# Output products of a gated layer: one issue list with fixed offsets, VectorE sums and some plain products

## The chip, the cores and the metric

One core of a Trainium2 chip runs the whole program. The metric is the device time of one execution in microseconds (us); less is better. Matrix products run on TensorE (PE, with its weight loads as PEld), elementwise work on VectorE (DVE), ScalarE (ACT) and GpSimd (POOL); SyncE (SP) issues nearly all DMAs, in program order.

## The reference

```python
x = attention with k and v averaged over blocks of 8          # 2304 tokens x 512
x = sum over e of p[:, e] * (relu(x @ w1[e]) @ w2[e])         # 4 experts, 512 -> 1024 -> 512
xn = x / sqrt(mean(x * x) + 1e-6) * rms_g
g = xn @ w_gate; val = xn @ w_val                             # 512 -> 1536
out = ((g * sigmoid(g)) * val) @ w_out                        # 1536 -> 512
```

All in float32. `w_gate`, `w_val` and `w_out` come as 64-bit words, which the kernel turns into float32 first.

## The kernel before

The 2304 tokens are three passes of 768. First come three expert stages (one for each pass, 8 quads each), then three gated stages (12 quads each: g and v for each of six rows of 256 hidden units). A quad (`quad`, L432) is a product of 2x2 blocks in Winograd's form of Strassen's scheme, with seven products instead of eight. Each float32 operand is split into a high and a low part, and a product is three matmuls (high by high, high by low, low by high), so a quad is seven steps of six 384-column matmuls. After each step the quad calls `hook`, which issues a share of everything else: gates, preparation of the next quad's weights, norms, conversions and DMAs. So the order on every in-order engine is written out by hand, a step at a time.

The PSUM tile qX is written at steps 0, 2, 4 and 6. Between them ACT copies it (L458, L461) and DVE adds it into `u` (L465). `gate_after` and `val_after` (L500, L521) leave four 384-column blocks of the gated value for each row in a tile `qq`.

The output product takes two rows at a time, also in Winograd's form: `products` (L548) forms the operands and `second_g` (L618) issues 14 units of six matmuls (M1, M2, M6, M7, M5, M4, M3, two halves each), 84 matmuls in all. M1, M2 and M3 use blocks of `qq` as they are (`rows`, L559). M6, M7, M5 and M4 need sums t1 and t2 (L580, L588, L591), which run on POOL. For the last pair they run on DVE and M3 is moved forward. Each operand is rounded to its high part on ACT (L562, L568), and DVE subtracts that to give the low part (L564, L569). M1's operand is formed at the end of the pair's second v quad, and the units follow evenly over the next 28 steps; those of the very last pair come after the last quad. Results are added into SBUF (`put_x` L636 and `put_y` L643 on DVE; on ACT, L634 and L641, for a pass's first pair), and L629 stores them.

The last expert product of the third pass (72 matmuls of 512 columns, `second`, L705, with sums at L727) is spread over the first four gated quads. `norm` (L749) then reads the sums back from DRAM (L765), scales them (L772), turns them on PE (L782) and stores them for the gated stages.

In pass 0 `prep_w` (L253) makes each gated quad's weights on POOL, ACT and DVE from a block loaded one quad ahead (L250) and stores them; later passes load them (L264, L265).

The conversion of the 64-bit weights (`convert_all`, L321) runs in the background of the expert stages. Each block is loaded to a tile `cr` (L336), with tag `rw` or `kr` by turns. For each of the six rows of `w_out`, `combine` (L382) makes seven weight blocks in high and low parts: sums on POOL (L387 to L390), high parts on ACT (L396), low parts on DVE (L399). `put` queues the store to `ws_d`, which SP issues two steps later (L241). The first four blocks lie in tiles of tags `aT` and `kr`, one buffer each, so the next load into `kr` waits until those stores have landed. `load_gw` (L537) reads `ws_d` back, into four buffers `w2` (L542).

Of the kernel before, what the change touches and what calls it, by code (L numbers as in the profile page):

```python
# [54 lines left out]
def tile_kernel(ctx: ExitStack, tc, qp, kp, vp, dp, w1r, w2r, w64, rg, out):  # L55
# [265 lines left out]
    def convert_all():  # L321
# [4 lines left out]
        halves = {}  # L326
# [15 lines left out]
        for n, (k, r_, c) in enumerate(keys):  # L342
# [39 lines left out]
    def combine(r, halves):  # L382
# [42 lines left out]

# [119 lines left out]

    M1, M2, M6, M7, M5, M4, M3 = range(7)

    def products(p, g, tail):  # L548

        qs = [gate_t.pop((p, 0, g * G + j)) for j in range(G)]  # L550
        eng = nc.vector if tail else nc.gpsimd
        ops = {}
        late_t = {}

        def new_op(n, tag, bufs):
            ops[n] = late["sb"].tile([P, 2, G, N], F32R, name="ho", tag=tag, bufs=bufs)
            return ops[n]

        def rows(n, k, tag="hA", bufs=4):  # L559
            o = new_op(n, tag, bufs)  # L560
            for j in range(G):
                nc.scalar.activation(o[:, 0, j], qs[j][:, k], AF.Copy)  # L562
            for j in range(G):
                nc.vector.tensor_tensor(o[:, 1, j], qs[j][:, k], f32(o[:, 0, j]), op=ALU.subtract)  # L564

        def sums(n, src):
            o = new_op(n, "hA", 4)
            nc.scalar.activation(o[:, 0], src, AF.Copy)  # L568
            nc.vector.tensor_tensor(o[:, 1], src, f32(o[:, 0]), op=ALU.subtract)  # L569

        def new_t():
            return late["sb"].tile([P, 2, G, N], F32, name="ht", tag="hB", bufs=3)

        def steps():
            rows(M1, 1)
            yield
            rows(M2, 3)
            t1 = new_t()
            for j in range(G):
                eng.tensor_tensor(  # L580
                    t1[:, :, j], qs[j][:, 0:1].to_broadcast([P, 2, N]), qs[j][:, 1:3], op=ALU.subtract
                )
            yield
            rows(M3, 2, "hB", 3)
            yield
            t2 = new_t()
            for j in range(G):
                eng.tensor_tensor(t2[:, 0, j], qs[j][:, 2], t1[:, 0, j], op=ALU.subtract)  # L588
            yield
            for j in range(G):  # L590
                eng.tensor_tensor(t2[:, 1, j], qs[j][:, 3], t2[:, 0, j], op=ALU.subtract)  # L591
            yield
            yield
            sums(M6, t2[:, 0])
            for _ in range(4):
                yield
            sums(M7, t1[:, 1])
            for _ in range(4):
                yield
            sums(M5, t1[:, 0])  # L600
            for _ in range(4):
                yield
            sums(M4, t2[:, 1])
            yield

        it = steps()
        next(it)

        def need(n):
            while n not in ops:  # L610
                next(it)
            return ops[n]

        return it, need

    ct = {}

    def second_g(p, g, need, tail):  # L618

        first, last = g == 0, g == R2 // G - 1  # L620
        x2 = late["pg"].tile([P, 2, 512], F32, name="gx", tag="gx")[:, :, :N]
        y2 = None
        if first:
            ct[0] = new_y(1).rearrange("p (j c n) -> p j c n", j=2, c=2)

        def out_of(i, j):
            if last:
                o = out[i * 256:(i + 1) * 256, p * TT * P + j * N:p * TT * P + (j + 1) * N]
                nc.sync.dma_start(o.rearrange("(c p) n -> p c n", c=2), ct[i][:, j])  # L629

        def put_x(i, j, fresh, z=None):
            d, z = ct[i][:, j], x2 if z is None else z
            if fresh and first:
                nc.scalar.activation(d, z, AF.Copy)  # L634
            else:
                nc.vector.tensor_tensor(d, z, d, op=ALU.add)  # L636

        def put_y(i, j, c, fresh, z):
            d = ct[i][:, j, c]
            if fresh and first:  # L640
                nc.scalar.activation(d, z, AF.Copy)  # L641
            else:
                nc.vector.tensor_tensor(d, z, d, op=ALU.add)  # L643

        order = (M1, M2, M3, M6, M7, M5, M4) if tail else (M1, M2, M6, M7, M5, M4, M3)
        for n in order:
            o = need(n)
            if n == M6 and first:
                ct[1] = new_y(0).rearrange("p (j c n) -> p j c n", j=2, c=2)
            if n in (M2, M7):  # L650
                y2 = [late["ps"].tile([P, 512], F32, name="gy", tag="py", bufs=2)[:, :N] for _ in range(2)]
            if n == M3 and tail:
                z2 = [late["ps"].tile([P, 512], F32, name="gz", tag="qX", bufs=2)[:, :N] for _ in range(2)]
            for c in range(2):
                w = gw[p, g, n // 2]
                z = y2[c] if n in (M2, M7, M4) else z2[c] if n == M3 and tail else x2[:, c]
                start = n in (M1, M2, M7) or n == M3 and tail
                for j in range(G):
                    wh, wl = (w[:, n % 2, j, i, c * P:(c + 1) * P] for i in range(2))
# [7 lines left out]
                elif n == M7:  # L667
                    put_y(1, 1, c, True, z)
                elif n == M4:
                    put_y(1, 0, c, False, z)  # L670
                elif n == M3 and tail:
                    put_y(0, 1, c, True, z)
                elif c:
# [606 lines left out]
```

## Time and profile before

| | |
|---|---|
| Median of 3 runs | 1314.22 us (1312.6 to 1317.47) |
| Profiled execution: time, span | 1311.7 us, 1309.9 us |
| PE, PEld busy | 1253.0 us (96%), 1152.8 us (88%) |
| DVE, ACT, POOL busy | 829.0 us (63%), 539.9 us (41%), 339.9 us (26%) |
| Mean granted TensorE clock | 0.987 of full speed |
| DMA | 342.27 MB, mean 261 GB/s |

The span runs from the first instruction to the last; the execution's own time has about 2 us around it. A matmul's duration is longer than the interval at which matmuls start, since they are pipelined, so that PE's busy time counts work that overlaps. Idle time of PE, and stretches at a lower clock, are what can be lost or won beside the number of matmuls.

### The profile page before, as it was taken

The page shows a single profiled execution, that of the slowest core. Times are in us where ns is not written, and L with a number is a line of the kernel's source. Part 1 is how long each engine was busy: PE and PEld are TensorE (multiplying, and loading weights), DVE is VectorE, ACT ScalarE, POOL GpSimd, SP SyncE. Part 2 cuts the span into 40 slices and gives each one's busy share as a digit, 9 for nine tenths or more (in the row PEclk, how much of TensorE's full clock was granted, in tenths as well). Part 3 has the DMA queues.
Part 4 walks back from the last instruction along what each step waited for, and adds up shares of the span by engine and source line. Part 5 has one row for each costly group of instructions (what it writes and reads, how often), then busy time and mean ns, then how long its engine had stood idle before and what let it go on. Part 6 is the DMA issues. An engine that isn't in the chain of part 4 may idle for free.

```text
span 1309.9 us, 18235 instructions
## 1 busy us (share of the span) xinstructions
PE 1253.0 (96%) x6836; PEld 1152.8 (88%) x6836; DVE 829.0 (63%) x1323; ACT 539.9 (41%) x1246; POOL 339.9 (26%) x301
## 2 busy tenths in 40 slices
PE   7899999999999999999998999999999999999995
PEld 6788898889888889889897888898988999999994
DVE  5864555557556665455766666567779556865655
ACT  5664444435443333233433332355454344433330
POOL 5234324310132222100332432134352022202200
PEclk8899999999999999999999999999999999999999
DMA  7296787768777776557979886667887776757651
GB/s 241 88 350 254 267 284 273 278 236 322 272 287 278 267 266 235 199 217 265 334 289 317 297 290 238 251 249 281 306 322 272 295 281 258 297 202 287 235 209 64
DMA packets 94135, 342.27 MB, mean 261 GB/s; under 512 B 9312, under 2 KB 32864, under 8 KB 73696
## 3 DMA queue, kind: packets, MB, share of 16 engines
q1 hardware_dynamic: 93712, 339.94, 71.3%
q10 hardware_dynamic: 336, 1.18, 0.3%
q8 instruction: 53, 0.87, 0.3%
q14 instruction: 34, 0.28, 0.1%
HBM read 238.33 MB, written 102.76 MB: 260 GB/s over the span
## 4 chain that ended last, share of the span: by engine, by line
PE 44%; DVE 8%; DMA 4%; issue 1%; ACT 1%; SPq 0%; POOL 0%; DVEq 0%; ACTq 0%; POOLq 0%
PE qX L453 5%; PE qX L455 5%; PE qX L454 5%; PE py L716 4%; PE py L717 4%; PE py L715 4%; PE qY L453 2%; PE qY L454 2%; PE qY L455 2%; DVE ho L564 2%; PE gx L663 2%; DMA ws_d<-oh 1%; DMA wt<-wt_d 1%; PE gx L664 1%; PE gx L662 1%; PE gy L663 1%
## 5 line engine op out<-in xcount | busy, mean ns | idle before, releaser
L727 DVE SCALAR_TENSOR_TENSOR y<-py,dps,y 128x512 f32<-128x512 f32 x126 | 94.5, 750 | 190.6 <-PE py L717 190.2
L371 POOL TENSOR_TENSOR cx<-cx,ca 128x512 f32<-128x512 f32 x36 | 49.2, 1367 | 394.8 <-DVE ca L369 166.5
L453 PE MATMUL qX<-xos,wt 128*128 128x384 f32 x336 | 116.3, 346 | 3.6 <-ACT qZ L458 2.6
L455 PE MATMUL qX<-xos,wt 128*128 128x384 f32 x336 | 114.3, 340 | 0.0
L717 PE MATMUL py<-w,hB 128*128 128x512 f32 x288 | 114.0, 396 | 0.0
L716 PE MATMUL py<-w,hB 128*128 128x512 f32 x288 | 113.9, 395 | 0.0
L454 PE MATMUL qX<-xos,wt 128*128 128x384 f32 x336 | 113.8, 339 | 0.0
L717 PE MATMUL py<-w,hA 128*128 128x512 f32 x288 | 113.4, 394 | 0.0
L716 PE MATMUL py<-w,hA 128*128 128x512 f32 x288 | 113.2, 393 | 0.0
L715 PE MATMUL py<-w,hB 128*128 128x512 f32 x288 | 112.8, 392 | 0.0
L715 PE MATMUL py<-w,hA 128*128 128x512 f32 x288 | 112.0, 389 | 0.0
L271 POOL TENSOR_TENSOR tw<-rw 128x512 f32<-128x512 f32 x28 | 41.7, 1488 | 236.5 <-DVE wt L288 147.7
L482 ACT ACTIVATE hB<-u 128x768 fp32r<-128x768 f32 x48 | 40.8, 850 | 144.4 <-DVE u L465 144.4
L461 ACT ACTIVATE s<-qX 128x384 f32<-128x384 f32 x85 | 41.8, 491 | 127.0 <-PE qX L455 127.0
L580 POOL TENSOR_TENSOR ht<-qq 128x768 f32<-128x768 f32 x16 | 31.2, 1948 | 211.0 <-DVE qq L527 113.2
L463 DVE TENSOR_TENSOR u<-qY,s 128x384 f32<-128x384 f32 x84 | 46.5, 553 | 41.8 <-PE qY L455 24.3
L453 PEld LDWEIGHTS qX<-xos,wt 128*128 128x128 f32 x336 | 63.5, 189 | 10.2 <-ACT qZ L458 4.7
L458 ACT ACTIVATE qZ<-qX 128x384 f32<-128x384 f32 x83 | 39.9, 481 | 77.4 <-PE qX L455 41.7
L454 PEld LDWEIGHTS qX<-xos,wt 128*128 128x128 f32 x336 | 63.8, 190 | 3.1
L717 PEld LDWEIGHTS py<-w,hB 128*128 128x128 f32 x288 | 54.3, 189 | 11.7
L717 PEld LDWEIGHTS py<-w,hA 128*128 128x128 f32 x288 | 54.0, 188 | 11.4
L455 PEld LDWEIGHTS qX<-xos,wt 128*128 128x128 f32 x336 | 63.6, 189 | 0.2 <-DVE wt L288 0.2
(187 smaller groups left out, 3587.7 us busy)
## 6 DMA issues: line engine op xcount, KB each, us to landing
wt<-wt_d SPq DMA_DIRECT2D x56, 1024.0 KB, 7.8
wr<-wr_d SPq DMA_DIRECT2D x56, 768.0 KB, 5.1
w<-w_d SPq DMA_DIRECT2D x32, 1024.0 KB, 10.2
wt_d<-wt SPq DMA_DIRECT2D x28, 1024.0 KB, 6.8
w<-ws_d SPq DMA_DIRECT2D x27, 1024.0 KB, 6.6
wr_d<-wr SPq DMA_DIRECT2D x28, 768.0 KB, 5.8
cr<-w SPq DMA_DIRECT2D x36, 512.0 KB, 5.4
w_d<-w SPq DMA_DIRECT2D x16, 1024.0 KB, 10.6
```

The source lines that it names most:

```text
L271: nc.gpsimd.tensor_tensor(t[:, T1:N3 + 1], r[:, B12:B12 + 1].to_broadcast([P, 2, 256]), r[:, B11:B22 + 1], op=sub)
L371: nc.gpsimd.tensor_tensor(x, x, m.bitcast(F32), op=ALU.mult)
L453: nc.tensor.matmul(bank[b], wh, xh, start=first and k == 0, stop=False, **kw)
L454: nc.tensor.matmul(bank[b], wh, xl, start=False, stop=False, **kw)
L455: nc.tensor.matmul(bank[b], wl, xh, start=False, stop=k == 1, **kw)
L461: nc.scalar.activation(s[n], bank[b], AF.Copy)
L463: nc.vector.tensor_tensor(u[:, 0], bank["Y"], s[2], op=ALU.add)
L482: nc.scalar.activation(h[:, 0], u, AF.Relu)
L715: nc.tensor.matmul(ps, lhs[0], w[:, 0, c], start=j == 0, stop=False)
L716: nc.tensor.matmul(ps, lhs[0], w[:, 1, c], start=False, stop=False)
L717: nc.tensor.matmul(ps, lhs[1], w[:, 0, c], start=False, stop=j == len(units) - 1)
L727: nc.vector.scalar_tensor_tensor(y_t[t], ps, gate, y_t[t], op0=ALU.mult, op1=ALU.add)
```

## The change

- A pass has a plan. Passes 0 and 1 take pairs of rows, pass 2 takes pairs (0, 1) and (2, 3) and then rows 4 and 5 one by one. Kind "s" is the scheme with seven products in 14 units. Kind "p" is a plain product with eight units: 12 matmuls each for a pair, 6 for a single row. The first two pairs of pass 0 and the last two rows of pass 2 are plain.
- A job for each plan entry is made before its last v quad. Its `prep` and its units have step numbers counted from that quad's end, from step -3 on: first unit at step 4 (single rows: 5), then every second step (plain pairs: every third; the last pair of pass 2 and single rows: every step). After the last quad the steps left run at once.
- All sums t1, t2 are on DVE, at steps 1 to 4 in six instructions.
- `combine` makes an eighth block (a21) for plain products. Its first two blocks lie in the unused half of the tile `cx` (tags `rw2` and `vr`), the next two in `aT`, and none in `kr`; a second tile of tag `es` is used.
- The last expert product of pass 2 is not spread any more: all of it runs after the second gated quad.
- The first weights of the output product are loaded four at a time, before the fourth gated quad; a plain row's weights come by two DMAs of 512 KB.
- Partial results are paired differently in their two SBUF tiles (C00 with C11, C01 with C10).

```diff
             if n % 2:
-                x = sba.tile([P, 1024], F32, name="cx", tag="vr")[:, :512]
+                xt = sba.tile([P, 1024], F32, name="cx", tag="vr")
             else:
-                x = main.tile([P, 1024], F32, name="cx", tag="rw2")[:, :512]
+                xt = main.tile([P, 1024], F32, name="cx", tag="rw2")
+            x = xt[:, :512]
...
                 halves[c] = x
+                spare[c] = xt[:, 512:].bitcast(F32R).rearrange("p (a n) -> p a n", a=2)
                 if c:
                     yield True
-                    yield from combine(r_, halves)
+                    yield from combine(r_, halves, spare)
...
-        src = (a11, a12, sm[:, 0], sm[:, 1], sm[:, 2], a22, sm[:, 3])
+        src = (a11, a12, sm[:, 0], sm[:, 1], sm[:, 2], a22, sm[:, 3], a21)
         one = sba.tile([P, 2, 2, 256], F32R, name="oh", tag="aT")
-        two = sba.tile([P, 2, 2, 256], F32R, name="oh", tag="kr")
-        t = [one[:, 0], one[:, 1], two[:, 0], two[:, 1]]
+        t = [spare[0], spare[1], one[:, 0], one[:, 1]]
...
-        t += [tile_of("q", 2), tile_of("q", 2), tile_of("es", 2)]
+        t += [tile_of("q", 2), tile_of("q", 2), tile_of("es", 2), tile_of("es", 2)]
         high(t[5], src[5])
+        high(t[7], src[7])
...
         low(t[5], src[5], 5)
+        low(t[7], src[7], 7)
...
-    gw = {}
-    gseq = [(p, g, t) for p in range(NPASS) for g in range(R2 // G) for t in range(4)]
-    gnext = [0]
+    plans = []
+    for p in range(NPASS):
+        if p == NPASS - 1:
+            plans.append([("s", (0, 1)), ("s", (2, 3)), ("p", (4,)), ("p", (5,))])
+        else:
+            plans.append([("p" if p == 0 and r < 4 else "s", (r, r + 1)) for r in range(0, R2, G)])
+    gseq = [
+        (p, kind, rows, t)
+        for p in range(NPASS) for kind, rows in plans[p] for t in (range(4) if kind == "s" else rows)
+    ]
+    gw, gnext = {}, [0]
 
     def load_gw(n):
         while gnext[0] < min(n, len(gseq)):
-            p, g, t = gseq[gnext[0]]
-            w = main.tile([P, 2, G, 2, 256], F32R, name="w2", tag="w2", bufs=4)
-            q = 2 if t < 3 else 1
-            nc.sync.dma_start(f32(w)[:, :q], ws_d[g, t, :, :q])
+            p, kind, rows, t = gseq[gnext[0]]
+            w = main.tile([P, 4 * DM], F32R, name="w2", tag="w2", bufs=4)
+            if kind == "s":
+                w = w.rearrange("p (q j i n) -> p q j i n", q=2, j=G, i=2)
+                q = 2 if t < 3 else 1
+                nc.sync.dma_start(f32(w)[:, :q], ws_d[rows[0] // G, t, :, :q])
+            else:
+                w = w.rearrange("p (k i n) -> p k i n", k=4, i=2)
+                g, j = divmod(t, G)
+                nc.sync.dma_start(f32(w)[:, :2], ws_d[g, 0, :, :, j])
+                nc.sync.dma_start(f32(w)[:, 2:], ws_d[g, 2:4, :, 1, j].rearrange("k p i n -> p k i n"))
             gw[gseq[gnext[0]]] = w
             gnext[0] += 1
...
+    def new_c(k):
+        t = new_y(1 - k).rearrange("p (j c n) -> p j c n", j=2, c=2)
+        ct[0, k], ct[1, 1 - k] = t[:, 0], t[:, 1]
+
+    def put_c(dst, z, fresh):
+        if fresh:
+            nc.scalar.activation(dst, z, AF.Copy)
+        else:
+            nc.vector.tensor_tensor(dst, z, dst, op=ALU.add)
...
+        def high(n, k, tag="hA"):
+            o = ops[n] = new_op(tag)
+            if k is None:
+                nc.scalar.activation(o[:, 0], src(n), AF.Copy)
+            else:
+                for j in range(G):
+                    nc.scalar.activation(o[:, 0, j], qs[j][:, k], AF.Copy)
+
+        def low(n, k):
+            o = ops[n]
+            if k is None:
+                nc.vector.tensor_tensor(o[:, 1], src(n), f32(o[:, 0]), op=ALU.subtract)
+            else:
+                for j in range(G):
+                    nc.vector.tensor_tensor(o[:, 1, j], qs[j][:, k], f32(o[:, 0, j]), op=ALU.subtract)
...
+        def t_one(j):
+            nc.vector.tensor_tensor(
+                ts[0][:, :, j], qs[j][:, 0:1].to_broadcast([P, 2, N]), qs[j][:, 1:3], op=ALU.subtract
+            )
+
+        def t_two(i):
+            for j in range(G):
+                a, b = (qs[j][:, 2], ts[0][:, 0, j]) if i == 0 else (qs[j][:, 3], ts[1][:, 0, j])
+                nc.vector.tensor_tensor(ts[1][:, i, j], a, b, op=ALU.subtract)
+
+        do(-1, high, M1, 1)
+        do(0, low, M1, 1)
+        do(0, high, M2, 3)
+        do(1, low, M2, 3)
+        do(1, new_t, 0)
+        do(1, t_one, 0)
+        do(2, t_one, 1)
+        do(3, new_t, 1)
+        do(3, t_two, 0)
+        do(4, t_two, 1)
+        for n, lo, k, tag in ((M6, 4, None, "hA"), (M7, 5, None, "hA"), (M5, 7, None, "hA"), (M4, 8, None, "hA"),
+                              (M3, 9, 2, "hB")):
+            rel = lo if n == M3 else max(lo, at_u[2 * n] - 7)
+            do(rel, high, n, k, tag)
+            do(rel + 1, low, n, k)
...
+                o = ops[n]
+                for c in range(2):
+                    z = y2[c] if n in (M2, M7, M4) else x2[:, c]
...
+                    if n in (M2, M7, M4):
+                        i, j = {M2: (0, 0), M7: (1, 1), M4: (1, 0)}[n]
+                        put_c(ct[i, j][:, c], z, first and n == M7)
+                    elif c:
+                        i, j = {M1: (0, 0), M6: (1, 0), M5: (1, 1), M3: (0, 1)}[n]
+                        put_c(ct[i, j], x2, first and n != M5)
+                    if c and last and n in (M2, M5, M4, M3):
+                        out_of(p, i, j)
+                    if c and n in (M2, M7, M4, M3):
+                        load_gw(gseq.index(key + (n // 2,)) + 5)
+                    yield
...
+        if len(rows) == 1:
+            do(-3, high, 0, 0)
+            do(-2, low, 0, 0)
+            for k in range(2):
+                do(-2 + k, high, 0, 1, k)
+                do(-1 + k, low, 0, 1, k)
+        else:
+            for n, (h, j) in enumerate(((0, 0), (0, 1), (1, 0), (1, 1))):
+                do(n - 1, high, j, h)
+                do(n, low, j, h)
...
+                        z = late["ps"].tile([P, 512], F32, name="gy", tag="py", bufs=2)[:, :N]
+                        for j, r in enumerate(rows):
+                            w, o = gw[p, "p", rows, r], ops[j, h]
+                            for k in range(2):
+                                wh, wl = (w[:, (0, 1, 3, 2)[2 * i + k], a, c * P:(c + 1) * P] for a in range(2))
+                                xh, xl = (o[:, a, k] for a in range(2))
+                                b, e = j + k == 0, j + k == len(rows)
+                                nc.tensor.matmul(z, wh, xh, start=b, stop=False)
+                                nc.tensor.matmul(z, wh, xl, start=False, stop=False)
+                                nc.tensor.matmul(z, wl, xh, start=False, stop=e)
+                        put_c(ct[i, 1 - h][:, c], z, first)
+                        if c and last:
+                            out_of(p, i, 1 - h)
+                        if h * i * c:
+                            load_gw(gseq.index((p, "p", rows, rows[-1])) + 5)
+                        yield
...
+    jobs, gstep = [], [0]
+
+    def new_job(p, r):
+        for n, (kind, rows) in enumerate(plans[p]):
+            if rows[-1] != r:
+                continue
+            if kind == "s":
+                job = strassen(p, rows, [4 + u * (1 if n and p == NPASS - 1 else 2) for u in range(14)], n == 0, r == R2 - 1)
+            else:
+                at_u = [4 + 3 * u for u in range(8)] if len(rows) > 1 else [5 + u for u in range(8)]
+                job = plain(p, rows, at_u, n == 0, r == R2 - 1)
+            jobs.append((gstep[0] + 7,) + job)
+
+    def run_jobs():
+        for start, prep, units, at_u in jobs:
+            for f in prep.pop(gstep[0] - start, ()):
+                f()
+        for start, prep, units, at_u in jobs:
+            while at_u and at_u[0] <= gstep[0] - start:
+                at_u.pop(0)
+                next(units)
+        jobs[:] = [j for j in jobs if j[1] or j[3]]
+        gstep[0] += 1
...
-                run(gops)
+                if not moe:
+                    run_jobs()
...
-            if not done and k != "v":
+            if k == "v":
+                new_job(p, r)
+            if not done and moe:
                 late_quad = i in ids[-4:] and si + 1 < len(stages)
-                nq = 2 if moe else 4
-                if tiles[0]:
-                    at_n, units = (1, 3, 5), TT
-                else:
-                    at_n, units = range(7), 14
-                shares = [
-                    (1.4 if late_quad and j >= 7 * (nq - 1) else 1) * (j % 7 in at_n) for j in range(7 * nq)
-                ]
+                shares = [(1.4 if late_quad and j >= 7 else 1) * (j % 7 in (1, 3, 5)) for j in range(14)]
                 slots[:] = [
-                    math.floor(units * (1 - sum(shares[:j + 1]) / sum(shares)) + 0.501) * (4 if tiles[0] else 1)
-                    for j in range(7 * nq)
+                    math.floor(TT * (1 - sum(shares[:j + 1]) / sum(shares)) + 0.501) * 4 for j in range(14)
                 ]
...
-            if si == NPASS and i == ids[2]:
-                load_gw(2)
+            if si == NPASS and i == ids[3]:
+                load_gw(4)
...
-            if k != "g":
+            if moe:
                 done.append(key)
+            elif i == ids[1]:
+                run(side, side_left[0])
...
-                    side.append(second(done, e == 0 and r == 1, last_e))
-                    side_left[0] = TT * 4
-                else:
-                    g = r // G
-                    tail = si == len(stages) - 1 and last_e
-                    load_gw(4)
-                    it, need = products(p, g, tail)
-                    gops.append(it)
-                    side.append(second_g(p, g, need, tail))
-                    side_left[0] = 14
...
-    run(side, side_left[0])
+    while jobs:
+        run_jobs()
```

## Rows read from the trace of the kernel before

**Rows 1.** Windows: us, busy us of each engine, PEclk, DMA share, GB/s.

```profile
1270.00:1276.40 6.40, 6.39 (x37) 6.07 (x36) 3.74 (x6) 1.48 (x4) 0.00 (x0) 1.00 0.45 164
1276.40:1310.00 33.60, 17.09 (x84) 14.37 (x84) 18.91 (x29) 3.97 (x7) 0.00 (x0) 1.00 0.17 62
```

**Rows 2.** Timeline, last quad and end: start us, duration us, engine, line, instruction.

```profile
1275.01 0.33 PE L455 MATMUL qX<-xos,wr 128*128 128x384 f32 x1
1275.38 0.56 DVE L529 TENSOR_TENSOR qq<-qq,qX 128x384 f32<-128x384 f32 x1 [0.48 <-PE qX L455]
...
1305.16 0.33 PE L662 MATMUL gy<-ho,w 128*128 128x384 f32 x1
1305.34 0.33 PE L663 MATMUL gy<-ho,w 128*128 128x384 f32 x1
1305.51 0.34 PE L664 MATMUL gy<-ho,w 128*128 128x384 f32 x1
1305.89 0.56 DVE L643 TENSOR_TENSOR y<-gy,y 128x384 f32<-128x384 f32 x1 [0.49 <-PE gy L664]
```

**Rows 3.** PE's waits between 860 and 1276 us: total, times, longest us.

```profile
PE gx L663 <- DVE ho L564: 8.0, 11, 1.5
PE qX L453 <- DVE u L465: 2.1, 2, 1.2
PE qY L453 <- DMA wt<-wt_d: 1.6, 2, 0.9
PE qX L453 <- ACT qZ L458: 1.2, 2, 0.7
PE qX L453 <- ACT s L461: 0.9, 1, 0.9
PE pt L782 <- DVE u L463: 0.6, 1, 0.6
PE gx L662 <- ACT ho L562: 0.4, 1, 0.4
```

**Rows 4.** Windows around two starts of a pair's products and one stop at 720 us.

```profile
905.00:910.00 5.00, 4.50 (x18) 4.18 (x18) 5.00 (x5) 1.89 (x4) 4.42 (x4) 0.69 0.93 345
1005.00:1010.00 5.00, 4.54 (x17) 4.54 (x18) 5.00 (x7) 1.12 (x2) 2.56 (x2) 0.66 0.86 323
715.00:720.00 5.00, 1.59 (x10) 1.27 (x8) 3.47 (x6) 1.73 (x4) 0.00 (x0) 0.92 1.02 399
720.00:725.00 5.00, 4.86 (x15) 4.48 (x16) 3.31 (x8) 0.51 (x2) 3.09 (x3) 0.50 1.03 421
```

**Rows 5.** Instructions of line L564: durations ns min/median/max, first and last start.

```profile
L564 DVE TENSOR_TENSOR ho<-qq,ho x54: 544/1220/1648, 903.6 to 1285.1; 128x384 fp32r<-128x384 f32 x54
```

**Rows 6.** Groups by line from 905 us: count, busy us, mean ns, idle before.

```profile
L569 DVE TENSOR_TENSOR ho<-ht,ho 128x768 fp32r<-128x768 f32 x36 | 35.4, 983 | 27.2 <-ACT ho L568 27.2
L580 POOL TENSOR_TENSOR ht<-qq 128x768 f32<-128x768 f32 x14 | 27.5, 1962 | 206.4 <-DVE qq L527 108.6 <-DVE ho L569 97.8
L643 DVE TENSOR_TENSOR y<-gy,y 128x384 f32<-128x384 f32 x48 | 26.6, 556 | 41.5 <-PE gy L664 41.3
L580 DVE TENSOR_TENSOR ht<-qq 128x768 f32<-128x768 f32 x2 | 1.8, 953 | 0.0
```

**Rows 7.** Timeline of SP's DMA issues, then of DVE, in the stop at 720 us.

```profile
701.90 1.87 SPq L88 DMA_DIRECT2D xs_d<-st  x2
711.20 0.34 SPq L336 DMA_DIRECT2D cr<-w  x1
713.07 0.78 SPq L336 DMA_DIRECT2D cr<-w  x1
716.53 0.43 DVE L360 TENSOR_SCALAR ca<-cr 128x512 uint32<-128x512 uint32 x1 [5.26 <-DMA cr<-w]
```

**Rows 8.** DMA issues by line: count, KB each, median us to landing.

```profile
w<-ws_d SPq DMA_DIRECT2D x27, 1024.0 KB, 6.6
rw<-wc_d SPq DMA_DIRECT2D x12, 512.0 KB, 5.5
```

More of the change, by code (lines that the diff above doesn't have):

```diff
@@ L325, in convert_all @@
         crs = {}
-        halves = {}
+        halves, spare = {}, {}
         def load(n):
@@ L546, in tile_kernel @@
     M1, M2, M6, M7, M5, M4, M3 = range(7)
-    def products(p, g, tail):
-        qs = [gate_t.pop((p, 0, g * G + j)) for j in range(G)]
-        eng = nc.vector if tail else nc.gpsimd
-        ops = {}
[L553 to L634, printed above, removed]
-            else:
[L636 to L641, printed above, removed]
-            else:
[L643 to L659, printed above, removed]
-                    xh, xl = (o[:, i, j] for i in range(2))
-                    kw = dict(skip_group_check=True)
-                    nc.tensor.matmul(z, wh, xh, start=start and j == 0, stop=False, **kw)
-                    nc.tensor.matmul(z, wh, xl, start=False, stop=False, **kw)
-                    nc.tensor.matmul(z, wl, xh, start=False, stop=j == G - 1, **kw)
-                if n == M2:
-                    put_y(0, 0, c, False, z)
[L667 to L673, printed above, removed]
-                    if n == M1:
-                        put_x(0, 0, True)
-                    elif n == M6:
-                        put_x(1, 0, True)
-                    elif n == M5:
-                        put_x(1, 1, False)
-                        if tail:
-                            put_x(0, 1, False)
-                    elif n == M3:
-                        put_x(0, 1, True)
-                if c:
-                    if n == M2:
-                        out_of(0, 0)
-                    elif n == M5:
-                        out_of(1, 1)
-                        if tail:
-                            out_of(0, 1)
-                    elif n == M4:
-                        out_of(1, 0)
-                    elif n == M3 and not tail:
-                        out_of(0, 1)
-                    if n % 2 == 1 or n == M3:
-                        load_gw(gseq.index((p, g, n // 2)) + 5)
-                yield
@@ new lines, in tile_kernel, with out_of @@
+    ct = {}
+    def new_c(k):
[6 more added lines that the diff above has]
+            nc.vector.tensor_tensor(dst, z, dst, op=ALU.add)
+    def out_of(p, i, j):
+        o = out[i * 256:(i + 1) * 256, p * TT * P + j * N:p * TT * P + (j + 1) * N]
+        nc.sync.dma_start(o.rearrange("(c p) n -> p c n", c=2), ct[i, j])
@@ new lines, in plain, with high, low, do @@
+    def plain(p, rows, at_u, first, last):
+        qs = [gate_t[p, 0, r] for r in rows]
+        ops = {}
+        prep = {}
+        def high(j, h, k=None):
+            if (j, h) not in ops:
+                ops[j, h] = new_op()
+            if k is None:
+                nc.scalar.activation(ops[j, h][:, 0], half(qs[j], h), AF.Copy)
+            else:
+                nc.scalar.activation(ops[j, h][:, 0, k], half(qs[j], h)[:, k], AF.Copy)
+        def low(j, h, k=None):
+            o = ops[j, h]
+            if k is None:
+                nc.vector.tensor_tensor(o[:, 1], half(qs[j], h), f32(o[:, 0]), op=ALU.subtract)
+            else:
+                nc.vector.tensor_tensor(o[:, 1, k], half(qs[j], h)[:, k], f32(o[:, 0, k]), op=ALU.subtract)
+        def do(rel, f, *args):
+            prep.setdefault(rel, []).append(lambda: f(*args))
+        if len(rows) == 1:
[8 more added lines that the diff above has]
+                do(n, low, j, h)
+        def units():
+            for h in range(2):
+                for i in range(2):
+                    if first and h == 0:
+                        new_c(1 - i)
+                    for c in range(2):
+                        z = late["ps"].tile([P, 512], F32, name="gy", tag="py", bufs=2)[:, :N]
[14 more added lines that the diff above has]
+                        yield
+        return prep, units(), at_u
```

41 lines of the change are left out of this document (35 added, 6 removed).

## The prediction

> **What bounds the kernel now.** First the windows, for where TensorE (PE) doesn't work at full speed; then the timeline there; then who waited for whom. The windows show a PE that is busy without a break through most of the span, so that a matmul more or less counts in full there: successive matmuls of 384 columns start 0.173 to 0.175 us apart [rows 2], so a step of six takes 1.04 us. Three places are different.
>
> The end: up to 1276.4 us PE is full, after it busy for 17.1 of 33.6 us [rows 1]. The last quad's last matmul starts at 1275.01 and the span ends at 1309.9, which is 34.9 us for 84 matmuls that alone would take 14.6; VectorE's (DVE's) last add ends at 1306.45, and 3.45 us follow it [rows 2].
>
> The starts of pairs: before the tail, PE's waits in the gated stages are led by L663 on L564, 8.0 us in 11 waits, and 0.4 for L662 [rows 3]. M1's low part is asked for right behind its high part. Two of these starts also halve the clock for a while: mean granted clock 0.69 and 0.66 in 5 us each, between levels 1.2 and 2.4 GHz [rows 4].
>
> The conversion in the third expert stage: around 720 us PE has 3.4 us of idle time and the clock falls, to 0.50 in the next five [rows 4].
>
> **The change part by part.** Changes in us against the profiled execution (1311.7, span 1309.9). The median of the runs is 2.5 above it; I add the sum to the median.
>
> *Matmuls.* A plain pair has 8 x 12 = 96 instead of 84, rows 4 and 5 together 2 x 8 x 6 = 96. So 36 more. Of 96 the tail keeps 48, where it had 84, so the part ahead of the tail gets 36 + 84 - 48 = 72 more: 72 x 0.1735 = **+12.5**. The Trainium skill (TensorE: Matmul & The Clock Gate, section "Wait — 56ns, not 53.3ns?") puts starts at columns over 2.4 GHz plus 2.5 ns, which is 162.5 ns here; the rows say 173 to 175, and they decide. By the rule the term would be 11.7.
>
> *Tail.* Row 5's units follow the last quad at once. Count from the start of its last matmul. The first half of `qq` is ready two steps earlier; its high part on ACT lies behind PE work, and its low part (0.95 to 0.98, as L569 without and with disturbance [rows 6]) ends about 0.2 us before zero. The other half waits for the last product: gate multiply 0.38 to 0.94 (as L529 [rows 2]), then two low parts of 0.55 [rows 5] and one add of 0.56 of row 4's last unit [rows 6], ready at about 2.1. The first four units (24 matmuls, 4.2 us) need only the first half, so it comes in time. Late next is the third unit: it wants the PSUM buffer of the first, whose add waits behind the low parts, about 0.4. So the last matmul starts at 8.3 + 0.4 = 8.7; add 0.38 and 0.56, and 3.45 to the end as now: 13.1 instead of 34.9, **-21.8**. If the low part comes one operation later it is 12 to 20 in place of 13.1; I keep 13.1, since each wait in it has a row.
>
> *Starts of pairs.* Units begin four steps behind the rows, over 4 us, where M1's operand needs two ACT copies and two subtracts. Gone: 8.4 us of idle time; some 0.27 for each of 12 waits, because a matmul that starts behind a wait leaves 0.1 more before the next and the one ahead of it drains for 0.16 (0.33 duration against 0.174 [rows 2]); and the clock, about (1 - 0.69) x 5 + (1 - 0.66) x 5 = 3.3: 8.4 + 3.2 + 3.3 = **-15**.
>
> *Late next at these starts.* The sums now queue on DVE in steps 0 to 2, ahead of L463 and L465, for which PE waits: lows of M1 and M2 4 x 0.55, t1 2 x 0.95 [rows 5, 6], the add of the previous pair's last unit 0.95, together 5.1 us in three steps and two units of PE, 5.2 us. L564 itself falls from a median of 1.22 to its minimum of 0.54, as POOL has no sums (L580 took 1.96 there, 0.95 on DVE [rows 6]). So up to 1 us late, of which the unit at step 4 hides most: 0.5 for each of six pairs, **+3**. Ends: 0, if the units hide it all, and +15, if nothing is won.
>
> *Start of the gated stage.* 72 expert matmuls leave the first four gated quads and run in one piece. For PE that is the same work, but four quads now run bare, 7.3 us each, while every one still prepares weights: ACT's copies and L465 must come within one step of 1.04 us. Five gaps of about 0.5 make 2.5. Then DMA: four weight loads of 1 MB are issued at the fourth quad, and SP's queue has the six stores of the norm and the read back (L765) ahead of them, which waits until its store has landed. At the 421 GB/s of the busiest window [rows 4] 4 MB take 10 us. The block of the next quad's weights (L250), issued behind, lands 5.5 us after issue in the median now [rows 8], and is wanted within 7.3. If it lands 4 us late, ACT stands still with PE's copies queued behind its own, and such a stop has cost its idle time again in clock [rows 4]: I take 4 in all. Sum **+6.5**. Ends: 0 (now nothing there waits for L250) and +13, two stops like that at 720 us. The Trainium skill (DMA: Bandwidth & Descriptors, section "Queues, rings and completion order") says that each DMA engine takes descriptors in ring order, which speaks for the late block; by ring order strictly kept the block would land about 12 us behind the issue and the term would be nearer 9. No row here shows it by itself.
>
> *Conversion.* The stop at 720 us: SP issues nothing from 703.8 to 711.2, and then the load into `kr`, whose buffer had to wait for stores of `combine`; DVE stood 5.26 us for that load, behind it what PE needed [rows 7]. After the change no store lies in `kr`; the load can go some 7 us earlier. But DMA was full (share 1.02 [rows 4]), so it may land only 3 or 4 us earlier. Of the 3.4 us idle and 3.4 of clock (0.92, 0.50 and a rest) I take **-5.5**. Added: a high part, a low part and a 256 KB store in each of six rows, hidden behind PE. The tile `cx` now waits for a store: ACT's next write there (L362) comes about 2 us behind the landing; without that cover ACT would wait, with qX copies behind it. Ends: -8.5 (a neighbouring wait goes too) and +2.
>
> *The other waits* of the gated stages, 6.4 us [rows 3], I leave as they are (ends -6 and +4): fewer operand copies in the plain pairs, denser units in pass 2, where two jobs take one step each.
>
> Sum: 12.5 - 21.8 - 15 + 3 + 6.5 - 5.5 = -20.3. Profiled execution 1291.4, median 1293.9; I say **1293**.
>
> **Rivals.**
> 1. *The tail alone counts.* PE waits as long as before, at other places: sums late at each pair, gaps at the stage's start, the conversion held up by full DMA queues. For it: DVE is in order and has more to do at four steps. Against: its share is 63%. -21.8 + 12.5 and 3 to 5 us won elsewhere: about 1302.
> 2. *All hidden.* Nothing new is late (terms +3 and +6.5 go), the 6.4 us go too and the conversion gives 8.5: -21.8 + 12.5 - 15 - 8.5 - 6 = -38.8, or 1276. For it: POOL no longer disturbs DVE. Against: four bare quads leave ACT and DVE no slack.
> 3. *Slower: the sums ahead of L465.* If at step 4 DVE is behind by more than the unit issued there covers (1.04 us), PE stops at step 6 in each of six pairs. A stop like that at 720 us costs 6.8: 6 x 6.8 = 41 in place of 3, so -20.3 + 38 = +17, about 1332. It decides from 4 us a pair on (6 x 4 = 24 cancels the gain). For it: 5.1 us of work in 5.2. Against: steps 3 and 4 give time to catch up, and a backlog of 4 us would need three more operations.
> 4. *The schedule doesn't do what it says at the end*: row 5's first units wait as the pair's did, and the tail takes 20 to 25 us: about 1303.
>
> **How the numbers follow.** Forecast 0.60, with its own range 1286 to 1300; rival 1 0.16, rival 2 0.13, rival 3 0.04, rival 4 0.07. About 0.5% (6.6 us) is what a measurement can tell from no change: faster ends at 1307.6. Forecast, rival 2 and most of rivals 1 and 4 lie under it: faster 0.89, same 0.07, slower 0.04. The range takes rivals 1 and 4 in, and half of rival 2: 1280 to 1306.
>
> **What would show it.** Right: no L663 wait on a low part of M1; under 14 us from the last quad's last matmul to the end; no SP gap ahead of a load into `kr`, and full clock around 720; 36 more matmuls. Wrong: PE waiting for L463 or L465 at steps 3 to 6 of a pair's first quad; ACT idle for L250 around the fifth gated quad with a clock at half; waits of L362 for `ws_d`. A span of more than 1302 would mean that one of the two middle gains was given back.

## The result and the profile after

The changed kernel takes 1293.94 us (median of 4 runs, 1293.07 to 1296.49), the kernel before, run beside it, 1313.41 (1308.79 to 1317.47). The ratio is 0.9856, 95% interval 0.982 to 0.9892. The forecast was 1293.0, range 1280 to 1306. The profiled executions, which the readings below compare, have spans of 1309.9 and 1291.3 us.

The page of the changed kernel: 36 more matmuls (6872 against 6836) in 18.6 us less.

```profile
span 1291.3 us, 18290 instructions
PE 1249.5 (97%) x6872; PEld 1154.1 (89%) x6872; DVE 809.3 (63%) x1340; ACT 537.2 (42%) x1239; POOL 270.9 (21%) x253
```

PE's waits in the gated stages, the view of [rows 3] for the changed kernel. The 8.0 us on a low part of M1 are gone; one wait of 8.5 us is new, and apart from it 3.9 us are left.

```profile
PE qX L455 <- ACT s L463: 9.6, 3, 8.5
PE qX L455 <- DVE u L467: 1.1, 2, 0.8
PE gx L654 <- DVE y L574: 0.9, 1, 0.9
PE qY L455 <- ACT s L463: 0.6, 1, 0.6
PE gy L721 <- DVE y L574: 0.2, 1, 0.2
```

The windows of [rows 4], and those around the new wait. At 720 us and at 1005 us the clock is now full (1.00, where it was 0.92, 0.50 and 0.66). From 905 to 910 no matmul starts, and the next 5 us run at half clock (0.50, the level of 1.2 GHz).

```profile
715.00:720.00 5.00, 4.46 (x23) 3.61 (x22) 3.30 (x7) 0.66 (x2) 3.26 (x3) 1.00 0.98 393
720.00:725.00 5.00, 4.66 (x22) 3.94 (x23) 3.98 (x7) 3.23 (x10) 2.48 (x4) 1.00 0.96 325
900.00:905.00 5.00, 2.54 (x15) 2.22 (x13) 2.34 (x3) 1.80 (x3) 0.00 (x0) 1.00 1.06 401
905.00:910.00 5.00, 0.00 (x0) 0.00 (x0) 0.00 (x0) 0.24 (x1) 0.13 (x1) 0.65 1.01 417
910.00:915.00 5.00, 3.96 (x12) 3.97 (x13) 4.36 (x6) 3.08 (x5) 3.81 (x3) 0.50 0.80 303
1005.00:1010.00 5.00, 4.32 (x25) 3.97 (x24) 5.00 (x9) 2.83 (x6) 0.00 (x0) 1.00 1.02 363
```

Two timelines of the changed kernel say what that wait is. SP's DMA issues: the output product's weights for four rows, eight loads of 512 KB, between 888.43 and 895.26; behind them, at 898.10, the 512 KB block of the next quad's weights.

```profile
888.43 0.52 SPq L558 DMA_DIRECT2D w<-ws_d  x1
...
895.26 0.65 SPq L559 DMA_DIRECT2D w<-ws_d  x1
896.26 0.54 SPq L241 DMA_DIRECT2D wt_d<-wt  x1
898.10 0.33 SPq L250 DMA_DIRECT2D rw<-wc_d  x1
```

ACT: it waits 7.96 us for that block (the bracket: idle before, and what ended it), and the copy L463, for which PE waits, is queued behind. The block landed 11.6 us after issue, against a median of 5.5 before [rows 8].

```profile
900.95 0.85 ACT L683 ACTIVATE ho<-qq 128x768 fp32r<-128x768 f32 x1
909.76 0.84 ACT L277 ACTIVATE wr<-rw 128x768 fp32r<-128x768 f32 x1 [7.96 <-DMA rw<-wc_d]
910.51 0.47 ACT L463 ACTIVATE s<-qX 128x384 f32<-128x384 f32 x1
```

The conversion at 720 us, which answers [rows 7]: the load of `cr` that DVE waits for is issued at 703.52 (was 711.20). DVE waits 1.68 us for it (was 5.26) and takes it up at 711.37 (was 716.53).

```profile
703.52 0.60 SPq L336 DMA_DIRECT2D cr<-w  x1
711.37 0.43 DVE L361 TENSOR_SCALAR ca<-cr 128x512 uint32<-128x512 uint32 x1 [1.68 <-DMA cr<-w]
```

The tail, as [rows 2]. The last quad's last matmul starts at 1278.22, row 5's units follow without a gap, PE waits once, and DVE's last add ends at 1287.96: 13.05 us to the end of the span, where it was 34.9.

```profile
1276.98 0.95 DVE L690 TENSOR_TENSOR ho<-qq,ho 128x768 fp32r<-128x768 f32 x1
1278.22 0.33 PE L457 MATMUL qX<-xos,wr 128*128 128x384 f32 x1
1278.39 0.33 PE L721 MATMUL gy<-ho,w 128*128 128x384 f32 x1
1279.06 1.23 DVE L692 TENSOR_TENSOR ho<-qq,ho 128x384 fp32r<-128x384 f32 x2
1280.30 0.34 PE L723 MATMUL gy<-ho,w 128*128 128x384 f32 x1
1280.82 0.45 PE L721 MATMUL gy<-ho,w 128*128 128x384 f32 x1 [0.18 <-DVE y L574]
1287.03 0.34 PE L723 MATMUL gy<-ho,w 128*128 128x384 f32 x1
1287.40 0.56 DVE L574 TENSOR_TENSOR y<-gy,y 128x384 f32<-128x384 f32 x1 [0.49 <-PE gy L723]
```

### The profile page after: what moved, and what is told of

It reads as the page before. It is cut to its first block, busy times and chain, and to the rows that moved or that the text cites. A ratio compares the mean times of both kernels' runs of the same rounds, so it can differ in the third digit from the quotient of the medians.

```text
span 1291.3 us, 18290 instructions
## 1 busy us (share of the span) xinstructions
PE 1249.5 (97%) x6872; PEld 1154.1 (89%) x6872; DVE 809.3 (63%) x1340; ACT 537.2 (42%) x1239; POOL 270.9 (21%) x253
## 4 chain that ended last, share of the span: by engine, by line
PE 51%; DVE 4%; DMA 2%; ACT 1%; issue 1%; POOL 0%; SPq 0%; ACTq 0%; DVEq 0%
PE qX L455 6%; PE qX L457 5%; PE qX L456 5%; PE py L774 4%; PE py L775 4%; PE py L773 4%; PE qY L455 3%; PE qY L457 3%; PE qY L456 3%; PE qZ L455 1%; PE gy L721 1%; PE qZ L457 1%; PE qZ L456 1%; PE gy L722 1%; PE gy L723 1%; PE gx L654 1%
## 5 line engine op out<-in xcount | busy, mean ns | idle before, releaser
L455 PE MATMUL qX<-xos,wt 128*128 128x384 f32 x336 | 116.4, 347 | 13.4 <-ACT s L463 11.2
L463 ACT ACTIVATE s<-qX 128x384 f32<-128x384 f32 x85 | 41.7, 490 | 126.7 <-PE qX L457 126.7
L465 DVE TENSOR_TENSOR u<-qY,s 128x384 f32<-128x384 f32 x84 | 46.5, 554 | 59.7 <-PE qY L457 32.7
L775 PEld LDWEIGHTS py<-w,hA 128*128 128x128 f32 x288 | 54.0, 188 | 11.4
L774 PEld LDWEIGHTS py<-w,hA 128*128 128x128 f32 x288 | 54.0, 188 | 10.1
## 6 DMA issues: line engine op xcount, KB each, us to landing
w_d<-w SPq DMA_DIRECT2D x16, 1024.0 KB, 10.7
```

The costliest lines, as they stand in the source:

```text
L455: nc.tensor.matmul(bank[b], wh, xh, start=first and k == 0, stop=False, **kw)
L463: nc.scalar.activation(s[n], bank[b], AF.Copy)
L465: nc.vector.tensor_tensor(u[:, 0], bank["Y"], s[2], op=ALU.add)
L774: nc.tensor.matmul(ps, lhs[0], w[:, 1, c], start=False, stop=False)
L775: nc.tensor.matmul(ps, lhs[1], w[:, 0, c], start=False, stop=j == len(units) - 1)
```

## The experiments

Below, a quad's time is the start of DVE's addition of `qY` into `u` behind its step 3 (L465; L463 in the kernel before), which each quad has once. Quads count from 0 through the program. An expert stage has 16 of them, not 8, so that the gated stages begin at quad 48; quad 83 is the last. All ratios are to the kernel before.

**e1_loads: the loads of the output product's weights away from the block.**

```diff
-            if si == NPASS and i == ids[3]:
-                load_gw(4)
+            if si == NPASS and i in (ids[2], ids[5]):
+                load_gw(2 if i == ids[2] else 4)
```

> The changed kernel, with the first four weight tiles of the output product loaded two before the third gated quad and two before the sixth, in place of four before the fourth. My theory: the stop of 8.5 us (and the half clock behind it) comes from ACT waiting for a weight block that lies behind 4 MB of these loads in full DMA queues. Then PE has no wait over 1.5 us in the gated stage, the clock stays full, and the time falls by 10 to 12 us, to 1282 to 1284. Rival: four bare quads are too short for ACT and VectorE whatever the DMAs do; then the stop stays, and the time is 1291 to 1295.

1284.66 us, ratio 0.9778 (0.9753 to 0.9804), 0.7 above the theory's range. PE has no wait over 0.9 us from 860 us on, and these are its windows where the stop was. From quad 51 to quad 53 it takes 19.8 us; the changed kernel takes 30.5. So the stop costs 10.7 us.

```profile
900.00:905.00 5.00, 4.58 (x26) 4.27 (x26) 4.65 (x6) 3.95 (x7) 3.19 (x3) 1.00 1.04 403
905.00:910.00 5.00, 5.00 (x30) 5.00 (x30) 5.00 (x8) 2.17 (x5) 0.94 (x1) 1.00 0.64 205
```

**e10_twoloads: half of the bytes ahead of the block.**

```diff
-            if si == NPASS and i == ids[3]:
-                load_gw(4)
+            if si == NPASS and i in (ids[3], ids[5]):
+                load_gw(2 if i == ids[3] else 4)
```

> As the changed kernel, but only expert weights of group 2 (2 MB) are issued at the third of the first four rows, and those of group 4 at the last: half as many bytes stand ahead of the 512 KB block that the gated stage's first conversion waits for. Theory (the stop at the start is this block's place behind the bytes issued ahead of it): it lands about 5 us earlier than in the changed kernel, the stop of 8.5 us shrinks to some 3.5 us, and the time is 1287 to 1289 us. Rival A (any load ahead of the block costs the whole stop): 1293 to 1295. Rival B (only the second load decides): the stop is gone, 1284 to 1286 us.

1289.6 us, ratio 0.9806 (0.9769 to 0.9843), just above the theory's range. The loads are of the output product's weights, as in e1_loads, not of expert weights. The block is issued at 900.66 and ACT takes it up at 909.08, 8.4 us behind the issue. Quad 51 to 53 takes 23.5 us, 3.7 more than e1_loads, with one wait of PE of 2.9 us. The theory holds, and shows two parts: with 2 MB less ahead the block lands 3.2 us sooner behind its issue (8.4 for 11.6), and it is issued 0.7 us behind quad 51 instead of 3.2. In e1_loads, with no such load ahead, that is 0.7 too, so four loads don't hold SP up there and eight do.

```profile
909.08 0.84 ACT L277 ACTIVATE wr<-rw 128x768 fp32r<-128x768 f32 x1 [2.32 <-DMA rw<-wc_d]
```

```profile
905.00:910.00 5.00, 2.50 (x15) 2.18 (x13) 2.35 (x4) 2.68 (x5) 0.81 (x1) 0.98 1.00 411
910.00:915.00 5.00, 4.64 (x19) 4.65 (x20) 5.00 (x7) 2.40 (x4) 3.12 (x3) 0.68 0.85 303
```

**e2_kr: the conversion's first blocks in `kr` again.**

```diff
-        t = [spare[0], spare[1], one[:, 0], one[:, 1]]
+        two = sba.tile([P, 2, 2, 256], F32R, name="oh", tag="kr")
+        t = [one[:, 0], one[:, 1], two[:, 0], two[:, 1]]
```

> The changed kernel, with the first four of combine's eight blocks back in tiles of tags aT and kr. My theory: SP's wait for the store in kr made the stop at 720 us; it comes back, with 5 us of waiting for the load on VectorE and the clock at half, and costs 4 to 5 us: 1298. Rival: the DMAs were full anyway and the buffer decides nothing: 1293 to 1295.

1300.51 us, ratio 0.9891 (0.9869 to 0.9914): 6.6 us over the changed kernel, where the theory had 4 to 5. The old picture is back: DVE waits 4.89 us for `cr` and PE 3.2, and the mean clock of the next 5 us is 0.70 (0.50 in the kernel before). From quad 39 to 45, the stretch of the stop, e2_kr takes 103.3 us, the kernel before 102.8 and the changed kernel 97.8.

```profile
716.01 0.43 DVE L361 TENSOR_SCALAR ca<-cr 128x512 uint32<-128x512 uint32 x1 [4.89 <-DMA cr<-w]
```

```profile
715.00:720.00 5.00, 1.81 (x11) 1.50 (x10) 3.95 (x8) 1.73 (x4) 0.00 (x0) 0.96 1.03 397
720.00:725.00 5.00, 5.00 (x20) 4.53 (x19) 3.33 (x6) 1.02 (x3) 3.53 (x4) 0.70 1.03 424
```

**e3_step1, e4_pool, e7_step1pool: the two parts of the new pair starts, one by one and together.** e3: units from one step behind the rows instead of four (the tail's pairs stay). e4: the sums on GpSimd again. e7: both, on top of e1_loads.

```diff
# e3
-[4 + u * (1 if n and p == NPASS - 1 else 2) for u in range(14)]
+[(1 if n == 0 or p < NPASS - 1 else 4) + u * (1 if n and p == NPASS - 1 else 2) for u in range(14)]
-at_u = [4 + 3 * u for u in range(8)]
+at_u = [1 + 3 * u for u in range(8)]
# e4, in both places
-nc.vector.tensor_tensor(
+nc.gpsimd.tensor_tensor(
```

> The changed kernel, with the first unit of every pair at step 1 in place of 4 (not in the last pair of pass 2 and the single rows). My theory: the offset of four steps removed the waits for M1's low part; at step 1 PE waits again at each of eight pairs, 0.5 to 1.5 us each, and the time is 1300 to 1304. Rival: the waits came from GpSimd's sums, which made VectorE's subtracts 1.22 us long in place of 0.55; with the sums on VectorE step 1 costs at most 2 us, 1294 to 1296.

> The changed kernel, with the sums t1 and t2 on GpSimd as before the change. They take about 9 us there (2 x 1.95 and 4 x 1.3) and M6's high part on ACT wants them at steps 4 to 6. My theory: ACT stands behind GpSimd with PE's copies queued behind it, 1 to 2 us at each of six pairs: 1300 to 1304. Rival: the offset alone is what counts and the engine of the sums doesn't matter: 1292 to 1296.

> The kernel of e1_loads (1284.7 us), with both the first unit at step 1 and the sums on GpSimd, as before the change. Each alone (e3_step1, e4_pool) made PE wait for a pair's operands at two pass boundaries only. My theory: the waits at the other starts need both, a unit one step behind its operand and a subtract made 1.2 us long by GpSimd; now seven or eight starts wait for a low part, 0.4 to 1.5 us each, and the time is 1297 to 1303. Rival: the starts within a pass don't wait in this issue order whatever the sums do: two or three waits, 1291 to 1296.

e3: 1298.41 us, ratio 0.9879 (0.9855 to 0.9903), +4.5 on the changed kernel, whose interval overlaps; from quad 48 to 83 it takes 420.1 us instead of 417.0, though its wait at the stage's start is 2.8 shorter (5.7 for 8.5). e4: 1303.85, ratio 0.9918 (0.9894 to 0.9943), +9.9; quads 48 to 83 +7.8. e7: 1295.81, ratio 0.9874 (0.9846 to 0.9901), 11.2 over e1_loads, in the same quads 8.8. Set against what was expected: e3 lies between its theory and its rival; e4 is in its theory's range, but with two stops instead of six; e7 is in its rival's range, with waits at four starts.

PE's waits in e3, from 860 us on: the low part of M1 is late again, but in two places only, the two boundaries between passes (at 1008.8 and 1146.0); other rows are the stop and two weight loads.

```profile
PE qX L455 <- ACT s L463: 5.7, 1, 5.7
PE qY L455 <- DMA wt<-wt_d: 2.6, 2, 1.4
PE gx L655 <- DVE ho L607: 1.9, 2, 1.2
```

In e7 it is 6.3 us in 5 waits, here between 990 and 1200 us (the kernel before has 5.0 in 7 there), at the two boundaries and at two starts inside passes.

```profile
PE gx L655 <- DVE ho L607: 6.3, 5, 3.2
```

e4 shows what the sums on GpSimd do to VectorE. Beside them two low parts take 2.64 us and an add of 128x768 1.74. ACT's L170 waits 4.42 us for that add, and PE at 1012.8 waits 4.29 for ACT's copy L463, which is queued behind L170: ACT stands behind VectorE, not behind GpSimd as the theory had it. The same happens at 1149.8 (3.8 us); at the four pair starts inside passes PE does not wait.

```profile
1006.45 5.94 POOL L623 TENSOR_TENSOR ht<-qq,ht 128x384 f32<-128x384 f32 x4
...
1007.23 2.64 DVE L607 TENSOR_TENSOR ho<-qq,ho 128x384 fp32r<-128x384 f32 x2
1009.79 1.74 DVE L207 TENSOR_TENSOR xr<-xr,xt 128x768 f32<-128x768 f32 x1
...
1011.57 0.84 ACT L170 ACTIVATE xos<-xr 128x768 fp32r<-128x768 f32 x1 [4.42 <-DVE xr L207]
1012.84 0.69 PE L455 MATMUL qX<-xos,wt 128*128 128x384 f32 x1 [4.29 <-ACT s L463]
```

The low parts alone, over the run: first the changed kernel (minimum, median, maximum in ns), then e3, with the sums on VectorE, then e4 (both with the mean in ns).

```profile
L607 DVE TENSOR_TENSOR ho<-qq,ho x36: 548/552/559, 1005.5 to 1245.3; 128x384 fp32r<-128x384 f32 x36
```

```profile
L607 DVE TENSOR_TENSOR ho<-qq,ho 128x384 fp32r<-128x384 f32 x36 | 18.4, 552 | 3.2 <-ACT ho L599 3.0
```

```profile
L607 DVE TENSOR_TENSOR ho<-qq,ho 128x384 fp32r<-128x384 f32 x36 | 32.8, 959 | 0.0
```

In e4 a low part with no GpSimd sum beside it takes 0.54 to 0.55 us, and one beside a sum of L623 takes 1.34 to 1.37 and ends 0.4 us behind that sum. The Trainium skill (SBUF — State Buffer, section "Who interferes with whom") says that a VectorE instruction with two inputs in SBUF contends with a GpSimd instruction that reads SBUF, and calls the ports that they share an exclusive lock. These durations agree with it.

Behind quad 58 the loads play no part: to quad 83 the changed kernel takes 285.3 us and e1_loads 285.4. There e3 loses 3.8 us, e4 8.9 and e7 6.4. So the later start gained nothing while GpSimd made the sums, the sums on VectorE gained 2.6 of the 6.4 without it, and the two together gained all. One profile of each stands behind this.

**e5_s0 and e9_mixed: fewer plain pairs in the first gated pass**, both on e1_loads; e5 has none there (24 matmuls fewer than e1), e9 has one instead of two (12 fewer).

```diff
-plans.append([("p" if p == 0 and r < 4 else "s", (r, r + 1)) for r in range(0, R2, G)])
+plans.append([("s", (r, r + 1)) for r in range(0, R2, G)])                              # e5
+plans.append([("p" if p == 0 and r < 2 else "s", (r, r + 1)) for r in range(0, R2, G)]) # e9
```

> The kernel of e1_loads (1284.7 us), with pass 0's first two pairs by the scheme with seven products like the others: 24 matmuls fewer, but three more operand copies and subtracts a pair and six sums on VectorE, while weights are being prepared. My theory: with the four-step offset nothing there waits for operands, and the matmuls count in full: -4.2 us, 1280 to 1281. Rival: VectorE and ACT are too full in pass 0, which is what the plain pairs are good for: PE waits take the gain back or more, 1284 to 1290.

> As e1_loads, but of the first four row blocks only the pair (0, 1) keeps its eight plain products per quad; the pair (2, 3) is a Strassen pair again (12 matmuls fewer). Theory (a plain pair costs its extra matmuls, nothing else, as long as the stage's first pair stays plain): 12 x 0.1735 = 2.1 us less than e1_loads, about 1282.5 us, with no stop of PE over 1.5 us at the stage's start. Rival (the sums of the Strassen pair come late behind the head's conversions and take the 2.1 us back, as they did with the whole of pass 0): 1284 to 1286 us, with a wait of 1 us or more on VectorE near quad 52.

e5: 1284.08 us, ratio 0.9784 (0.976 to 0.9809). e9: 1285.45, ratio 0.9782 (0.9754 to 0.981). Both are level with e1_loads. From quad 48 to 83 e1_loads takes 406.4 us, e5 404.1 and e9 405.5: of 4.2 us saved in matmuls 2.2 show, of 2.1 0.8. Up to quad 58 e5 wins 3.4, with a wait of 2.4 us on L467 at 911.3 against it, and e9 1.9; in both 1.0 to 1.1 come back behind it, around 1002 us, where PE waits 0.8 for an add. In the medians neither can be seen: the plain pairs of the first pass cost 1 or 2 us at most. In both the time is the rival's; e9's longest wait on VectorE, 1.6 us, is at 958.2, well behind quad 52, where the rival had it. The two rows of e9's waits from 860 us on:

```profile
PE qX L455 <- DVE u L467: 2.4, 3, 1.6
PE gx L654 <- DVE y L574: 1.7, 2, 0.9
```

**e6_pairtail: the last two rows as a Strassen pair**, on e1_loads.

```diff
-            plans.append([("s", (0, 1)), ("s", (2, 3)), ("p", (4,)), ("p", (5,))])
+            plans.append([("s", (0, 1)), ("s", (2, 3)), ("s", (4, 5))])
```

> The kernel of e1_loads (1284.7 us), with pass 2's last two rows as a pair by the scheme with seven products, as before the change: 12 matmuls fewer in all, 84 in place of 48 behind the last quad. My theory: the part ahead of the tail gets 48 x 0.1735 = 8.3 us shorter, the tail goes from 13.1 to 25 to 32 us because sums, subtracts and adds run in a chain on VectorE: +4 to +10, 1289 to 1295. Rival: units issued together keep PE full and the tail is no longer than its 84 matmuls and 5 us, 20 us: 1283 to 1284.

1290.41 us, ratio 0.9827 (0.9802 to 0.9852), 5.7 over e1_loads, as the theory had it. From the last quad's last matmul (1258.56) to the end it takes 27.2 us instead of 13.0; the part up to that matmul is 10.6 shorter. PE stands 3.09 us there and then runs at half clock. The profile names no releaser for that wait ("issue"). The matmul starts 0.10 us behind the end of DVE's add out of `gx`, the PSUM tile that it writes, of which there is one buffer; that add had queued behind four low parts and two sums.

```profile
1261.27 1.82 DVE L616 TENSOR_TENSOR ht<-qq 128x768 f32<-128x768 f32 x2
1263.01 0.95 DVE L574 TENSOR_TENSOR y<-gx,y 128x768 f32<-128x768 f32 x1
1264.06 0.66 PE L654 MATMUL gx<-ho,w 128*128 128x384 f32 x1 [3.09 <-issue]
```

The windows of the end:

```profile
1258.00:1264.00 6.00, 2.97 (x18) 2.65 (x16) 5.52 (x10) 1.32 (x3) 0.00 (x0) 0.92 0.73 262
1264.00:1270.00 6.00, 5.94 (x19) 5.97 (x20) 4.49 (x7) 2.42 (x3) 0.00 (x0) 0.51 0.00 0
```

So the plain end keeps only part of what it gains: 14.2 us at the end are bought with 10.6 ahead of it. The kernel before took 34.9 us behind the last quad for the same 84 matmuls, so that of the tail's gain some 7.7 us came without the plain rows and 14.2 with them.

**e8_spread: the 72 expert matmuls spread over the first four gated quads again**, on e1_loads.

```diff
+            if si == NPASS and i == ids[0]:
+                slots[:] = [4 * (TT - sum(m % 7 in (1, 3, 5) for m in range(j + 1)) // 2) for j in range(28)]
-            elif i == ids[1]:
+            elif i == ids[3]:
```

> The kernel of e1_loads (1284.7 us), with the last expert product of pass 2 spread over the first four gated quads again in place of one piece after the second. My theory: the same matmuls in either order, and bare quads cost no more than the 1.3 us that e1_loads still shows there: 1283 to 1286. Rival: the one piece lets the DMAs and the norm get ahead; spread, the buffers of the output weights come free later and the first loads again stand in the way: 1288 to 1296.

1286.34 us, ratio 0.9796 (0.9773 to 0.9819): not told apart from e1_loads (0.9753 to 0.9804), and below the rival's range. Running them in one piece costs nothing measurable once no load stands ahead of the block.

## Why the prediction was right

The time is right to a microsecond; the terms are not all. Measured by the times of quads in the two profiled spans:

- *Tail*, forecast -21.8, measured 34.9 - 13.05 = **-21.85**. Its steps came as put: the low part of the first half ends 0.29 us before the zero point (0.2 forecast), the second half is ready at 2.07 (2.1), the third unit starts 0.35 late (0.4), and 3.3 us follow the last add (3.45). Rival 4 falls.
- *Matmuls*: 36 more, 72 of them ahead of the tail. Starts lie 0.1735 apart in the rows of the tail above, as in [rows 2], so +12.5 stands as a price. It was not measured by itself; the nearest is e9_mixed, which wins 1.9 of 2.1 up to quad 58.
- *Conversion*, forecast -5.5: **-4.2**, the difference at quad 48 less that at quad 39 (-5.8 against -1.6). From quad 39 to 45 alone it is -5.0; the rest is lost between quads 45 and 46, where profiles differ anyway (last section). Undoing it alone gave +6.6. The load went out 7.7 us earlier (some 7 forecast), and DVE took it up 5.2 earlier, of which 1.6 is the program's start (3 or 4 forecast). The other part was lost in DMA, as put: its share is 1.02 from 705 to 710 us, and the load took 7.7 us to land, against 5.3 before. `cx` made no wait.
- *Start of the gated stage*, forecast +6.5 with 4 for the block: this is the term that was mis-sized. The block alone cost **10.7** (e1_loads). What I got wrong is its lateness: I put it 4 us late, counting from a need 7.3 us behind the issue, but SP issued it only at 898.10, behind the loads, and ACT was ready for it at 901.80, 3.7 us later, and stood 7.96. I gave more weight to the median landing time of a queue without such loads than to the queue in which the block would stand. One of the forecast's own signs of being wrong appeared here: ACT idle for L250 with the clock at half. The 11.6 us to its landing agree with descriptors taken in ring order (the Trainium skill, DMA: Bandwidth & Descriptors, "Queues, rings and completion order"), for which the prediction had put about 12.
- *Pair starts, late next and other waits*: forecast -15, +3 and 0, together with the 2.5 for bare quads -9.5. Quad 48 to the last quad's last matmul took 413.8 us before and 422.8 after, +9.0. Less 12.5 for matmuls and 10.7 for the block that leaves **-14.2**. e7_step1pool, which puts both parts of the new starts back, gives 8.8 of it back in quads 48 to 83; where the other 5.4 come from is not shown. The pair waits went entirely, as put, and L607 fell to the 0.55 us that L564's minimum had shown [rows 5]. Of +3 for late sums 2.0 showed, at the two starts behind a pass boundary: 0.9 for an add behind L616 (L654) and 1.1 for L467 behind L623, as below. Of the 6.4 us of other waits, kept at nothing, 1.7 are left. Which share the bare quads have is not told apart.

```profile
1011.32 1.02 DVE L623 TENSOR_TENSOR ht<-qq,ht 128x384 f32<-128x384 f32 x2
1012.25 0.56 DVE L467 TENSOR_TENSOR u<-qX,s 128x384 f32<-128x384 f32 x1
```

- *Program's start*: 1.6 us of the span's difference lie ahead of quad 39, 1.5 of them ahead of quad 0, where nothing was changed. The same code reaches quad 0's time at 62.0 to 65.6 us over the runs here.

Sum: -21.85 + 12.5 + 10.7 - 14.2 - 4.2 - 1.6 = -18.65, against 18.6 between the spans (it has to agree, since -14.2 is what the others leave) and a forecast of -20.3. So two errors, 6.7 too little for the block and 4.7 too little for the waits, mostly cancelled. The mechanism held where a run tested it: the tail, the conversion, the block's lateness, the pairs' waits. The total was in part luck.

Rival 1 (all waits stay) misses by 8 us, 1302 against 1293.9. One thing it named rightly: PE's waits between 860 us and the tail fell only from some 15 to 12.2 us, as 8.5 of them moved to the stage's start. Rival 2 (nothing new late) describes e1_loads, which is 9.3 us faster by moving the loads; its 1276 stays out of reach even so. Rival 3's waits for the old L465, now L467, are 0.8 and 0.4 us at two pairs; stops of about 4 us come, at two of six pairs, only when GpSimd makes the sums (e4_pool).

The best versions measured are e1_loads at 1284.66 and e5, e8 and e9, which are not told apart from it.

## What to carry to other kernels

Ask of each bulk load which small, urgent load is issued behind it: 4 MB ahead of 512 KB stopped the pipeline for 10.7 us, and moving the issues, half of them one quad earlier and half two quads later, gave 9.3 us back. An end that no later work covers is worth more plain work ahead of it, if its operands come in halves, each ready before the units that use it. Moving the sums off GpSimd paid in part by itself; starting the units later paid only on top of that.

## What the runs showed of the hardware

- A stop costs more than its length, but not twice, as the forecast had taken from [rows 4]: PE's wait of 8.5 us cost 10.7, with the clock at 0.50 in the 5 us behind it, and the 2.9 us of e10_twoloads cost 3.7, with 0.68 there.
- A low part of 128x384 on VectorE, 0.55 us alone, took 1.34 to 1.37 us in e4_pool beside a GpSimd sum.
- The same instructions do not always take the same time: between quads 45 and 46, which none of these edits touches, e3_step1 and e9_mixed lost 3.6 and 3.5 us more than e1_loads, around 816 us, where PE waits for weights. One profile against another can't settle less than that without looking at where the difference lies. Other stretches repeat far better: from quad 0 to 39 the kernel before and all others here take 644.7 us, within 0.1.
